# Moving twelve first additions of softmax weights to GpSimd, and folding the second batch's sums once more

## The chip, the cores and the metric

The kernel runs on one core of one Trainium2 chip. The metric is the device time of one execution in microseconds (us); for a kernel that ran several times, the median.

## The reference

Two layers, one after the other. The first is attention with a hash mask for 4 batches, 8 heads, 768 positions and 64 columns per head; the second is a feed-forward layer whose hidden values are the maximum of three products.

```
bits   = (q @ proj > 0), (k @ proj > 0)          # 6 bits each, a bucket per row
scores = q @ k.T / 8, -1e9 where the buckets of query and key differ
attn   = exp(scores - max) / (sum(exp(scores - max)) + 1e-9)
x      = attn @ v, heads side by side            # 3072 x 512
h      = maximum(x @ w1, x @ w2, x @ w3)          # 3072 x 768
out    = h @ w_out                                # 3072 x 512, float32
```

## The kernel before

**Units.** The queries are cut into nine chunks: three of 256 queries for batch 0 (chunks 0, 1, 2), and two of 384 for each of the others (3 and 4 for the second batch, 5 and 6 for the third, 7 and 8 for the fourth). A unit is 768 weights per partition of one chunk and one head: `scores` (line 281) issues its matmuls into PSUM (line 297), and one ScalarE exponential writes the weights in fp16 to one of 24 tiles `AT` (line 305). A chunk of 384 queries has three units per head, n = 0, 1, 2, each with two blocks of 128 keys. There are 192 units in all; units 48 to 95 are the second batch.

**The denominators.** A softmax row needs the sum of its weights over all 768 keys. It is taken by matmuls with a column block of ones (line 357, in `burst`), four heads at a time in four column groups. From chunk 3 on, VectorE first adds weights together in `add` (line 321): the addition n = 1 makes `ad` from the tiles of units 0 and 1 (line 328, `ad<-AT,AT`), the addition n = 2 adds the third tile (line 328, `ad<-ad,AT`), each over 768 columns. For chunks from `THIRD_ADD` on, a third addition puts the two halves of `ad` together, over 384 columns (line 331). `sum_blocks` then hands `burst` one block a head (chunks 5 to 8) or two (chunks 3 and 4). `ad` has five buffers.

**Order.** The order of every engine's queue is written out by hand in the loop over units (line 616). In slot u the kernel issues the scores of unit u + 1, then what `when` has put into the slot, then one or so pieces of the feed-forward layer, then the burst of four heads when one is due. The additions of unit (c, h, n) stand in slot u + 2, after everything else that `when` put there, so the additions n = 1 and n = 2 of one head are one slot apart. A burst of the second batch stands four slots after its last unit.

**The other work of the queues.** The feed-forward pieces use one of four PSUM banks in turn (line 412); VectorE takes them out (line 421, from chunk 3 on line 417 on ScalarE for the first of three products; line 419 before that). VectorE also transposes q and k of coming batches (line 201, `turn`) and makes the reciprocal sums and normalized rows (lines 364 to 386). GpSimd has three kinds of work after the start: it narrows transposed q and k to bf16 (line 206, `narrow`), issues the loads of q and k (line 195) and issues those of v (line 239). SyncE's queue holds the transfers out of the narrowed tiles (`place`) and the output.

Of the kernel before, what the change touches and what calls it, by code (L numbers as in the profile page):

```python
# [12 lines left out]
AluOp = mybir.AluOpType  # L13
# [4 lines left out]
def kernel(  # L18
# [12 lines left out]
    nc = tc.nc  # L31
# [20 lines left out]
    EPS = 2.0 ** -60  # L52
    NAT = 24
    SPREAD = {2: (61, 9), 3: (100, 12)}
    THIRD_ADD = 5
    LAG = (1, 4)
    ATW = 776

# [215 lines left out]
    def blocks(t, w):  # L274
        nb = 2 * HALF // w
        return t[:, 0 : nb * (w + 2)].rearrange("p (n c) -> p n c", n=nb)
# [32 lines left out]
    def weights_of(c, h, m):  # L309
        w = chunks[c][2]  # L310
        nb = 2 * HALF // w
        return blocks(at_tiles[at_of[unit_at[c, h, m // nb]]], w)[:, m % nb, :]
# [6 lines left out]
    sum_of = {}  # L319

    def add(c, h, n):
        w = chunks[c][2]
        t = [blocks(at_tiles[at_of[unit_at[c, h, i]]], w)[:, :, 0:w] for i in range(n + 1)]
        if n == 1:
            sum_of[c, h] = ad_pool.tile([P, 2, HALF], FP16, tag="ad", name="ad")
        else:
            t[0] = sum_of[c, h][:]
        nc.vector.tensor_tensor(out=sum_of[c, h][:], in0=t[0], in1=t[n], op=AluOp.add)  # L328
        if n == 2 and c >= THIRD_ADD:
            t = sum_of[c, h]  # L330
            nc.vector.tensor_tensor(out=t[:, 0, :], in0=t[:, 0, :], in1=t[:, 1, :], op=AluOp.add)  # L331

    def sum_blocks(c, h):
        w = chunks[c][2]
        if (c, h) in sum_of:
            t = sum_of[c, h]
            return [t[:, j, 0:w] for j in range(1 if c >= THIRD_ADD else 2)]
        return [weights_of(c, h, m)[:, 0:w] for m in range(NM)]
# [146 lines left out]
    with tc.manual_schedule():  # L485
# [126 lines left out]
        for u, (c, h, n) in enumerate(units):  # L612
            if c >= 3 and n:
                when(min(u + 2, NU - 1), add, c, h, n)
# [58 lines left out]
```

## Time and profile before

| | before |
|---|---|
| median of 3 runs | 266.32 us (265.26 to 266.48) |
| the profiled execution | 265.27 us, span 263.1 us |
| TensorE (PE) busy | 256.4 us, 97% |
| VectorE (DVE) busy | 208.5 us, 79% |
| ScalarE (ACT) busy | 177.4 us, 67% |
| GpSimd (POOL) busy | 70.1 us, 27% |
| additions of line 328 | 96, on VectorE |
| third additions of line 331 | 32, on VectorE |

An engine's busy time is the time in which at least one of its instructions ran; instructions that follow each other overlap by some hundredths of a microsecond, so start-to-start times are shorter than durations. The profiled execution is one run; its span runs from the first to the last instruction of the program, and its time is 2.2 us longer. The second batch's units run from about 55 to 111 us in the span.

### The profile page before, as it was taken

The page shows a single profiled execution, that of the slowest core. Times are in us where ns is not written, and L with a number is a line of the kernel's source. Part 1 is how long each engine was busy: PE and PEld are TensorE (multiplying, and loading weights), DVE is VectorE, ACT ScalarE, POOL GpSimd, SP SyncE. Part 2 cuts the span into 40 slices and gives each one's busy share as a digit, 9 for nine tenths or more (in the row PEclk, how much of TensorE's full clock was granted, in tenths as well). Part 3 has the DMA queues.
Part 4 walks back from the last instruction along what each step waited for, and adds up shares of the span by engine and source line. Part 5 has one row for each costly group of instructions (what it writes and reads, how often), then busy time and mean ns, then how long its engine had stood idle before and what let it go on. Part 6 is the DMA issues. An engine that isn't in the chain of part 4 may idle for free.

```text
span 263.1 us, 6495 instructions
## 1 busy us (share of the span) xinstructions
PE 256.4 (97%) x2509; PEld 153.6 (58%) x2509; DVE 208.5 (79%) x494; ACT 177.4 (67%) x257; POOL 70.1 (27%) x132
## 2 busy tenths in 40 slices
PE   7999999999999999999999999999999999999994
PEld 3555666866765666555555555555555555554552
DVE  3897766967799999978999997999759795887451
ACT  3697885667968675956869588584886859581322
POOL 4678752355043526331131612011000000000000
PEclk9999999999999999999999999999999999999999
DMA  6999999969832954970073653802030003000303
GB/s 173 306 247 193 173 251 222 203 114 206 207 91 69 205 141 62 268 188 18 0 209 93 119 123 48 208 1 62 15 122 1 0 2 121 2 0 2 120 0 120
DMA packets 20862, 30.95 MB, mean 118 GB/s; under 512 B 2625, under 2 KB 15393, under 8 KB 20833
## 3 DMA queue, kind: packets, MB, share of 16 engines
q0 software_dynamic: 8128, 13.37, 27.1%
q1 hardware_dynamic: 12192, 16.73, 22.0%
q10 hardware_dynamic: 512, 0.46, 0.5%
q8 instruction: 19, 0.31, 0.5%
q14 instruction: 11, 0.08, 0.1%
HBM read 25.17 MB, written 6.29 MB: 120 GB/s over the span
## 4 chain that ended last, share of the span: by engine, by line
PE 88%; DVE 5%; ACT 2%; issue 1%; DMA 1%; POOL 1%; ACTq 0%; DVEq 0%
PE ms L412 34%; PE sc L297 22%; PE ms L460 11%; PE ms L379 10%; PE ms L220 3%; PE ms L357 3%; ACT AT L305 2%; DMA nat<-in_q_dram 1%; PE ms L123 1%; PE ms L170 1%; DVE S L175 1%; DVE ht L421 1%; DVE ad L328 1%; PE ms L150 1%; POOL S L137 1%
## 5 line engine op out<-in xcount | busy, mean ns | idle before, releaser
L305 ACT ACTIVATE AT<-sc 128x768 f16<-128x768 f32 x192 | 152.6, 816 | 59.4 <-PE sc L297 56.1
L412 PE MATMUL ms<-xT,w_sb 128*128 128x384 f16 (+1 forms) x648 | 114.8, 307 | 0.1
L297 PE MATMUL sc<-S 72*128 72x384 bf16 (+1 forms) x432 | 93.6, 308 | 1.6 <-ACT AT L305 0.7
L412 PEld LDWEIGHTS <-w_sb 128*128 128x128 f16 x648 | 62.7, 97 | 35.9 <-issue 0.4
L421 DVE TENSOR_TENSOR ht<-ht,ms 128x384 f16<-128x384 f16 (+1 forms) x108 | 54.2, 503 | 21.7 <-PE ms L412 11.3
L297 PEld LDWEIGHTS <-S 72*128 72x128 bf16 (+1 forms) x432 | 39.4, 98 | 33.7 <-issue 13.5
L206 POOL TENSOR_SCALAR T<-T 128x768 bf16<-128x768 f32 x24 | 22.9, 954 | 90.3 <-issue 47.5
L460 PE MATMUL ms<-wout_sb,ht 128*128 128x512 f16 x138 | 35.5, 378 | 0.0
L379 PE MATMUL ms<-AT,vo 128*32 128x385 f16 (+3 forms) x840 | 34.4, 308 | 0.1
L328 DVE TENSOR_TENSOR ad<-ad,AT 128x768 f16<-128x768 f16 x48 | 26.5, 552 | 2.1 <-ACT AT L305 1.3
L379 PEld LDWEIGHTS <-vo 128*32 128x32 f16 x864 | 22.4, 96 | 9.5 <-issue 1.6
L201 DVE STREAM_TRANSPOSE T<-nat 128x384 f32<-128x384 f32 x48 | 26.8, 563 | 0.0
L328 DVE TENSOR_TENSOR ad<-AT,AT 128x768 f16<-128x768 f16 x48 | 26.2, 545 | 0.2 <-ACT AT L305 0.2
L417 ACT CAST ht<-ms 128x384 f16<-128x384 f32 x36 | 17.3, 480 | 8.1 <-PE ms L412 8.1
L460 PEld LDWEIGHTS <-ht 128*128 128x128 f16 x138 | 13.3, 97 | 13.0 <-issue 0.3
L386 DVE SCALAR_TENSOR_TENSOR xT<-ms,sv,rb 128x384 f16<-128x384 f32 (+1 forms) x35 | 19.2, 565 | 1.3
L464 ACT COPY osb<-ms 128x512 f32<-128x512 f32 x21 | 12.3, 586 | 7.1 <-PE ms L460 5.8
L331 DVE TENSOR_TENSOR ad<-ad 128x384 f16<-128x384 f16 x32 | 15.5, 484 | 1.1
L137 POOL TENSOR_SCALAR S<-T 64x384 bf16<-64x384 f32 (+1 forms) x23 | 14.2, 619 | 5.8 <-DVE T L132 4.4
L364 DVE STREAM_TRANSPOSE ys<-ms 128x384 f32<-128x384 f32 (+1 forms) x17 | 9.0, 531 | 6.3 <-PE ms L357 6.2
L195 POOL DMA_DIRECT2D nat<-in_q_dram x20 | 11.1, 561 | 0.1
L175 DVE TENSOR_SCALAR S<-ms 6x384 bf16<-6x384 f32 x16 | 8.9, 554 | 2.2 <-PE ms L170 1.8
(52 smaller groups left out, 122.1 us busy)
## 6 DMA issues: line engine op xcount, KB each, us to landing
out_dram<-osb SPq DMA_DIRECT2D x21, 256.0 KB
S<-T SPq DMA_DIRECT2D x48, 96.0 KB
nat<-in_q_dram POOLq DMA_DIRECT2D x20, 192.0 KB, 6.4
vo<-in_v_dram POOLq DMA_DIRECT2D x8, 384.0 KB, 5.9
nat<-in_k_dram POOLq DMA_DIRECT2D x16, 192.0 KB, 5.9
w_sb<-in_moe_w_dram POOLq DMA_DIRECT2D x3, 768.0 KB, 12.3
nat<-in_k_dram SPq DMA_DIRECT2D x10, 192.0 KB
nat<-in_k_dram SPq DMA_DIRECT2D x3, 384.0 KB
```

The costliest lines, as they stand in the source:

```text
L137: nc.gpsimd.tensor_scalar(out=o, in0=i_, scalar1=RS, scalar2=1.0, op0=AluOp.mult, op1=AluOp.mult)
L201: nc.vector.transpose(t32[name][:, u, half * HALF : (half + 1) * HALF], i_)
L206: nc.gpsimd.tensor_scalar(out=t16[name][:, u, :], in0=t32[name][:, u, :], scalar1=RS, scalar2=1.0, op0=AluOp.mult, op1=AluOp.mult)
L297: nc.tensor.matmul(views[j], s_of[kn][0 : D + bits, kx, m * P : (m + 1) * P], s_of[qn][0 : D + bits, qx, q0 : q0 + w], start=True, stop=True)
L305: nc.scalar.activation(t[:, :, 0:w], whole, ActFn.Exp, bias=-SCALE * 0.25 * bits, scale=SCALE)
L328: nc.vector.tensor_tensor(out=sum_of[c, h][:], in0=t[0], in1=t[n], op=AluOp.add)
L379: nc.tensor.matmul(av[Q * x : Q * (x + 1), 0:n], v_at[2 * b + i][:, x, cb * D + side : (cb + 1) * D : 2], weights_of(c, 4 * i + x, m)[:, 0 ...
L386: nc.vector.scalar_tensor_tensor(out=xt_of(c)[:, 2 * i + side, 0:w], in0=av[:, 0:w], scalar=sv_of[b, i, side][:], in1=rb[0][:, 0:w], op0=A ...
L412: nc.tensor.matmul(ps[:, 0:w], w_sb[wi][:, jc, fb * P : (fb + 1) * P], xt[:, jc, 0:w], start=(jc == 0), stop=(jc == NJC - 1))
L417: nc.scalar.copy(hts[fb][:, 0:w], ps[:, 0:w])
L421: nc.vector.tensor_tensor(out=hts[fb][:, 0:w], in0=hts[fb][:, 0:w], in1=ps[:, 0:w], op=AluOp.max)
L460: nc.tensor.matmul(ps[:, 0:DM], hts[fb][:, tb * P : (tb + 1) * P], wout_sb[:, fb, :], start=(fb == 0), stop=(fb == NFB - 1))
```

## The change

`THIRD_ADD` becomes 3, so that the sixteen heads of chunks 3 and 4 get the third addition too, and their bursts read one block a head in place of two. In the same chunks, the addition n = 1 of heads 0, 1, 2 and 4, 5, 6 (three of four) goes to GpSimd's queue, in the slot where it stood in VectorE's. The additions n = 2 and the third additions stay on VectorE.

```diff
-    THIRD_ADD = 5
+    THIRD_ADD = 3
...
-        nc.vector.tensor_tensor(out=sum_of[c, h][:], in0=t[0], in1=t[n], op=AluOp.add)
+        eng = nc.gpsimd if n == 1 and c < 5 and h % 4 < 3 else nc.vector
+        eng.tensor_tensor(out=sum_of[c, h][:], in0=t[0], in1=t[n], op=AluOp.add)
         if n == 2 and c >= THIRD_ADD:
             t = sum_of[c, h]
             nc.vector.tensor_tensor(out=t[:, 0, :], in0=t[:, 0, :], in1=t[:, 1, :], op=AluOp.add)
```

## The prediction

> **What bounds the kernel now.** I read the page's busy line first, then the table of stretches for the second batch, then the chain of waits there.
>
> ```profile
> span 263.1 us, 6495 instructions
> PE 256.4 (97%) x2509; PEld 153.6 (58%) x2509; DVE 208.5 (79%) x494; ACT 177.4 (67%) x257; POOL 70.1 (27%) x132
> ```
>
> TensorE is busy for 97% of the span, VectorE for 79%. An average hides stages, so the stretch that the change touches is looked at by itself (columns: length, then busy time and instructions of PE, PEld, DVE, ACT, POOL, the granted clock, the DMA share and GB/s).
>
> ```profile
> 70.00:110.00 40.00, 39.86 (x407) 25.65 (x405) 38.51 (x94) 28.81 (x40) 15.34 (x21) 1.00 0.59 134
> ```
>
> From 70 to 110 us VectorE is busy for 38.51 of 40 us. It has 1.49 us to spare, and TensorE has 0.14. Both are full, at a granted clock of 1.00, and GpSimd is busy for 15.34. The chain that ended last shows which of the two carries the end (columns: start, duration, what):
>
> ```profile
> 98.66 0.44 PE ms L412 x4
> 99.10 0.33 PE sc L297 x2
> 99.43 0.44 PE ms L412 x4
> ```
>
> Here TensorE runs back to back, and a slot with one feed-forward piece takes 99.43 - 98.66 = 0.77 us. So TensorE is the bound, with VectorE just able to follow. A wait put into VectorE's queue is free only as far as the 1.49 us go, plus the lead that the PSUM banks give.
>
> **What TensorE saves.** The four bursts of the second batch lose half of their sum matmuls, eight become four. Both forms are in the trace (columns: start, duration, then engine, line, operation and count): the first pair of rows is a burst of the second batch, the other one of the third.
>
> ```profile
> 73.17 0.51 PE L357 MATMUL ms<-ad,ones 128*32 128x384 f16 x8
> 73.50 2.15 PE L379 MATMUL ms<-AT,vo 128*32 128x385 f16 x48
> ...
> 132.28 0.35 PE L357 MATMUL ms<-ad,ones 128*32 128x384 f16 x4
> 132.45 2.15 PE L379 MATMUL ms<-AT,vo 128*32 128x385 f16 x48
> ```
>
> Start to start, eight take 73.50 - 73.17 = 0.33 us and four take 0.17. Four bursts save 4 x 0.16 = 0.64 us. That is on the path, and it is nearly all that can be won, since TensorE has only 0.14 us of idle time in the stretch.
>
> **What VectorE's own work becomes.** Between 70 and 110 us the trace has these additions, on VectorE:
>
> ```profile
> L328 DVE TENSOR_TENSOR ad<-AT,AT x12: 510/536/552, 70.1 to 109.5; 128x768 f16<-128x768 f16 x12
> L328 DVE TENSOR_TENSOR ad<-ad,AT x11: 515/516/993, 71.4 to 108.1; 128x768 f16<-128x768 f16 x11
> ```
>
> Of the twelve n = 1 additions, three (heads 3 and 7 of chunk 3, head 3 of chunk 4) stay, and nine go to GpSimd. The eleven n = 2 additions stay, and each gets a third addition behind it. What one costs in the queue is read from start to start:
>
> ```profile
> 81.97 0.55 DVE L328 TENSOR_TENSOR ad<-AT,AT 128x768 f16<-128x768 f16 x1
> 82.44 0.41 DVE L421 TENSOR_TENSOR ht<-ht,ms 128x256 f16<-128x256 f16 x1
> ...
> 120.30 0.52 DVE L328 TENSOR_TENSOR ad<-ad,AT 128x768 f16<-128x768 f16 x1
> 120.85 0.36 DVE L331 TENSOR_TENSOR ad<-ad 128x384 f16<-128x384 f16 x1
> 121.13 1.21 DVE L421 TENSOR_TENSOR ht<-ht,ms 128x384 f16<-128x384 f16 x2
> ```
>
> A large addition holds the queue for 0.47 us. One with a third addition behind it holds it for 121.13 - 120.30 = 0.83, so the third one costs 0.36. Removed are 9 x 0.47 = 4.2 us and added are 11 x 0.36 = 4.0. I call that zero: VectorE's queue is as full as before.
>
> **What the GpSimd additions do to VectorE.** The trace has no two-input instruction on GpSimd, but it shows what a one-input one does to VectorE's additions. GpSimd's narrowing alone, and twice beside a VectorE addition:
>
> ```profile
> 36.85 0.83 POOL L206 TENSOR_SCALAR T<-T 128x768 bf16<-128x768 f32 x1 [0.48 <-DVE T L201]
> ...
> 84.75 0.98 POOL L206 TENSOR_SCALAR T<-T 128x768 bf16<-128x768 f32 x1 [2.55 <-issue]
> ...
> 124.19 0.98 POOL L206 TENSOR_SCALAR T<-T 128x768 bf16<-128x768 f32 x1 [10.27 <-issue]
> ```
>
> ```profile
> 84.53 0.52 DVE L328 TENSOR_TENSOR ad<-AT,AT 128x768 f16<-128x768 f16 x1
> 85.15 0.99 DVE L328 TENSOR_TENSOR ad<-ad,AT 128x768 f16<-128x768 f16 x1
> ...
> 124.51 0.86 DVE L331 TENSOR_TENSOR ad<-ad 128x384 f16<-128x384 f16 x1
> ```
>
> The addition at 85.15 meets a GpSimd operation that ends at 85.73, and itself ends at 86.14 after 0.99 us in place of 0.52. The third addition at 124.51 meets one that ends at 125.17, and ends at 125.37 after 0.86 in place of 0.36. In both cases VectorE's addition does its work after the GpSimd operation has ended. The other way round, the narrowing that starts inside the addition at 84.53 takes 0.98 in place of 0.83. The two exclude each other. The group of third additions says how often:
>
> ```profile
> L331 DVE TENSOR_TENSOR ad<-ad 128x384 f16<-128x384 f16 x32 | 15.5, 484 | 1.1
> L331 DVE TENSOR_TENSOR ad<-ad x32: 357/358/866, 120.9 to 238.1; 128x384 f16<-128x384 f16 x32
> ```
>
> Mean 484 against median 358 over 32 is 4.0 us, or eight hits of 0.51.
>
> These rows do not say whether a GpSimd addition with two inputs excludes VectorE's for its whole length. The Trainium skill, SBUF — State Buffer, section "SBUF: two separate sides", says that the pair of ports common to both engines goes to the first comer for a whole instruction, and names VectorE operations with two SBUF inputs among those that block; by that rule the sum below holds, and without it the second rival does.
>
> How long is a GpSimd addition, X? One pass over 768 elements takes 0.83 us. Two inputs read together would also take 0.83, the low end; two passes take 1.66, which I use, as the operation reads twice as much; two passes with the delay of the colliding narrowing, 1.05 at most by the row at 99.90 quoted below, take 2.1, the high end. The Trainium skill, GPSIMD Engine Reference, section "Performance versus the Vector engine", gives 4497 ns for 2048 fp32 elements; an estimate scaled from that is 1.69 us, by which the sum would end 0.3 us higher.
>
> Some encounters can be followed one by one (ScalarE's row is the unit that releases head 4's addition on GpSimd):
>
> ```profile
> 70.16 0.81 ACT L305 ACTIVATE AT<-sc 128x768 f16<-128x768 f32 x1
> ```
>
> ```profile
> 71.40 0.52 DVE L328 TENSOR_TENSOR ad<-ad,AT 128x768 f16<-128x768 f16 x1
> ...
> 80.35 0.52 DVE L328 TENSOR_TENSOR ad<-ad,AT 128x768 f16<-128x768 f16 x1
> ...
> 93.51 0.52 DVE L328 TENSOR_TENSOR ad<-ad,AT 128x768 f16<-128x768 f16 x1
> ...
> 99.74 0.52 DVE L328 TENSOR_TENSOR ad<-ad,AT 128x768 f16<-128x768 f16 x1
> ```
>
> ```profile
> 80.52 1.05 POOL L206 TENSOR_SCALAR T<-T 128x768 bf16<-128x768 f32 x1 [3.85 <-DVE T L201]
> ...
> 92.39 0.59 POOL L195 DMA_DIRECT2D nat<-in_q_dram  x1
> ...
> 99.90 1.05 POOL L206 TENSOR_SCALAR T<-T 128x768 bf16<-128x768 f32 x1 [3.58 <-DVE T L201]
> ```
>
> Head 4 of chunk 3: its weights are there at 70.97, GpSimd is free, and its addition runs until 72.6. Head 3's n = 2 addition, at 71.40 on VectorE, waits 1.2 us for it. Head 1 of chunk 4: GpSimd's queue is held by a narrowing and a load issue until 92.98, so its addition ends at 94.64. VectorE reaches the n = 2 addition that needs the result at 93.51 and waits 1.1 us. Behind VectorE's waiting instruction stand the evacuations of lines 419 and 421; TensorE waits for their banks.
>
> For all of them I take chance encounters. Nine GpSimd additions in 40 us are one every 4.44 us. A VectorE addition that comes at any moment meets one with chance X / 4.44 and waits X / 2 on average. There are 25 of them in the stretch: 3 + 11 + 11. So 25 x 1.66 x 1.66 / (2 x 4.44) = 7.8 us (1.9 for X = 0.83, 12.4 for 2.1).
>
> The new third additions meet narrowings too, 0.51 us each. A narrowing starts inside an n = 2 addition three times in the stretch, the first at 80.52 and the last at 99.90 above; the third addition follows 0.55 us after the second, so it falls inside the narrowing: 1.5 us.
>
> Against these 9.3 us stand VectorE's spare 1.5 us and the banks' lead, which I bound by nothing and by two slots and take as one slot, 0.8 us, once. What is left, 7.0, is lost by TensorE, which has no idle time to give it back.
>
> **Moved and hidden.** GpSimd's loads fall behind additions in its queue. The four at 61.97 move behind two of them, 3.3 us later; the first VectorE transpose that needs them comes 20 us later, with a landing time of 6.4 us.
>
> ```profile
> 61.97 2.19 POOL L195 DMA_DIRECT2D nat<-in_q_dram  x4
> nat<-in_q_dram POOLq DMA_DIRECT2D x20, 192.0 KB, 6.4
> 82.77 0.57 DVE L201 STREAM_TRANSPOSE T<-nat 128x384 f32<-128x384 f32 x1
> ```
>
> If that cover were gone, the price would be the shift itself, 3.3 us. GpSimd's load in the stretch becomes 15.34 + 9 x 1.66 = 30.3 of 40 us, so its queue holds. The transfers of `place` on SyncE's queue only follow the narrowings; five `ad` buffers are enough, as a burst frees four of them while the next head's are made. I cost these at nothing.
>
> **The sum.** 7.8 + 1.5 - 1.5 - 0.8 - 0.6 = +6.4 us. On the profiled execution, 265.27, that gives 271.7; it lies 1.05 below the median of the runs, 266.32, so the median should be 272.7. The ends of X give +0.5 (266.8) and +11.0 (277.3).
>
> **Rivals.** *Half the encounters.* The phases are not random: the additions start when ScalarE has ended, and several find VectorE on evacuations for their whole length. With half of 7.8 the sum is +2.5: 268.8. For it: GpSimd's additions come some two slots before their results are needed. Against: two of the encounters above cost over 1 us each. *No exclusion by two-input additions.* Only waits for results remain, of which the walk above shows 1.1 us, and the spare 1.5 us hide them. Then TensorE's saving stands alone: 265.7, not slower. The case decides itself where all of VectorE's new waits stay under 1.5 + 0.8 = 2.3 us. Against it are the eight hits of 0.51. *GpSimd becomes the late one.* With X of 2.1 and more its load passes 34 of 40 us, narrowings come late, and every n = 2 addition waits for its first: 277.3 or above. Against it: a one-input pass takes 0.83. That the edit reaches other heads than said is excluded by its conditions: lines 328 and 331 count 96 and 32 before, and must count 84 on VectorE plus 12 on GpSimd, and 48.
>
> **How the numbers follow.** The forecast has 0.62, half the encounters 0.17, no exclusion 0.13, a late GpSimd 0.08. The range from 267.0 to 276.5 holds the first two, and leaves out the last two, 0.21. A measurement tells about 0.5%, or 1.33 us, from no change: no exclusion counts as the same (0.12) but for a small part that measures faster (0.02); the rest is slower (0.86).
>
> **What would show it.** In the profile after, twelve GpSimd additions of about 1.7 us; VectorE additions beside them that last 1 to 2.5 us; VectorE's busy share in the second batch at its full, and TensorE's idle time there up by 6 to 7 us; the bursts' sum matmuls in fours. I am wrong if the additions of line 328 on VectorE keep their 0.52 us beside GpSimd's, or if TensorE's idle time stays under 1 us.

## The result and the profile after

The changed kernel takes 276.93 us (median; 276.29 to 277.11), the kernel before on the same chip 266.09. The ratio is 1.040, 95% interval 1.038 to 1.043: 10.8 us slower. The forecast was 272.7 with a range from 267.0 to 276.5, so the direction was right and the size was not: the sum said +6.4, and the range ended 0.4 us too low.

Line numbers behind the edit are one higher in the changed kernel: line 329 is the large addition, 332 the third one, 413 and 422 the feed-forward matmuls and their evacuation. The page's first lines, and the same stretch as before (length, then busy time and instructions of PE, PEld, DVE, ACT, POOL, the granted clock, the DMA share, GB/s):

```profile
span 275.3 us, 6484 instructions
PE 261.1 (95%) x2493; PEld 155.6 (57%) x2493; DVE 219.9 (80%) x498; ACT 177.4 (64%) x257; POOL 89.3 (32%) x144
```

```profile
70.00:110.00 40.00, 34.16 (x296) 21.84 (x296) 36.61 (x80) 22.02 (x29) 19.87 (x21) 0.91 0.38 93
```

TensorE, at 39.86 of 40 us before, stands for 5.84 us in this stretch, and its granted clock is 0.91 where it was 1.00. VectorE is busy for 36.61 us, not fuller than before as forecast: it now waits too. By the start of each unit's exponential, all of the loss lies between units 60 and 96; from unit 104 on the two kernels keep a constant distance.

The additions by instruction (minimum, median and maximum in ns):

```profile
L329 DVE TENSOR_TENSOR ad<-ad,AT x48: 507/548/1984, 64.2 to 249.7; 128x768 f16<-128x768 f16 x48
L329 DVE TENSOR_TENSOR ad<-AT,AT x36: 515/551/1297, 72.6 to 249.1; 128x768 f16<-128x768 f16 x36
L329 POOL TENSOR_TENSOR ad<-AT,AT x12: 1632/1648/1709, 62.5 to 121.3; 128x768 f16<-128x768 f16 x12
...
L332 DVE TENSOR_TENSOR ad<-ad x48: 357/358/2450, 66.2 to 250.3; 128x384 f16<-128x384 f16 x48
```

The edit did what it says: 84 large additions on VectorE, 12 on GpSimd, 48 third ones. A GpSimd addition takes 1.65 us. VectorE's additions reach 1.98, 1.30 and 2.45 us.

The costliest episode, on GpSimd's queue, on VectorE's, and on TensorE's (whose first two rows are from another place, the first burst):

```profile
97.41 1.03 POOL L206 TENSOR_SCALAR T<-T 128x768 bf16<-128x768 f32 x1 [2.88 <-DVE T L201]
98.51 0.58 POOL L195 DMA_DIRECT2D nat<-in_q_dram  x1
99.11 3.24 POOL L329 TENSOR_TENSOR ad<-AT,AT 128x768 f16<-128x768 f16 x2
```

```profile
100.80 1.98 DVE L329 TENSOR_TENSOR ad<-ad,AT 128x768 f16<-128x768 f16 x1 [0.47 <-POOL ad L329]
```

```profile
75.93 0.35 PE L358 MATMUL ms<-ad,ones 128*32 128x384 f16 x4 [1.06 <-DVE ht L420]
76.55 3.71 PE L380 MATMUL ms<-AT,vo 128*32 128x385 f16 x48 [0.27 <-DVE ht L422]
...
103.56 0.95 PE L413 MATMUL ms<-xT,w_sb 128*128 128x256 f16 x4 [2.40 <-DVE ht L422]
```

A narrowing and a load issue hold GpSimd's queue, so two additions run back to back from 99.11 to 102.35. VectorE waits for the first one's result, and the second has begun when it comes: its addition starts at 100.80 and ends at 102.78, 0.43 us after GpSimd's. TensorE has no free bank and stands for 2.40 us. What follows such a stand is in the table by single microseconds (the granted clock is the figure third from the end):

```profile
78.00:79.00 1.00, 1.00 (x19) 0.55 (x12) 0.90 (x4) 0.00 (x0) 0.94 (x3) 0.50 0.00 0
...
102.00:103.00 1.00, 0.00 (x0) 0.00 (x0) 0.97 (x2) 0.07 (x1) 0.35 (x1) 1.00 0.28 74
...
105.00:106.00 1.00, 1.00 (x6) 0.70 (x5) 0.97 (x4) 0.76 (x1) 0.24 (x1) 0.50 0.06 16
```

In this execution TensorE's clock is halved for some 3.4 us, once around 78 and once around 105. The forty-eight matmuls of line 380 take 3.71 us in the first of these, where they took 2.15.

### The profile page after: what moved, and what is told of

Its sections match the earlier page's. It is cut to its first block, busy times and chain, and to the rows that moved or that the text cites. A ratio compares the mean times of both kernels' runs of the same rounds, so it can differ in the third digit from the quotient of the medians.

```text
span 275.3 us, 6484 instructions
## 1 busy us (share of the span) xinstructions
PE 261.1 (95%) x2493; PEld 155.6 (57%) x2493; DVE 219.9 (80%) x498; ACT 177.4 (64%) x257; POOL 89.3 (32%) x144
## 4 chain that ended last, share of the span: by engine, by line
PE 80%; DVE 9%; issue 3%; ACT 3%; POOL 2%; DMA 1%; ACTq 0%; DVEq 0%; POOLq 0%
PE ms L413 31%; PE sc L297 20%; PE ms L380 11%; PE ms L461 9%; DVE ad L329 3%; PE ms L220 3%; PE ms L358 3%; ACT AT L305 3%; DVE ad L332 1%; DMA nat<-in_q_dram 1%; POOL ad L329 1%; PE ms L123 1%; PE ms L170 1%; DVE S L175 1%; DVE T L201 1%
## 5 line engine op out<-in xcount | busy, mean ns | idle before, releaser
L413 PE MATMUL ms<-xT,w_sb 128*128 128x384 f16 (+1 forms) x648 | 116.1, 310 | 4.8 <-DVE ht L422 3.5
L422 DVE TENSOR_TENSOR ht<-ht,ms 128x384 f16<-128x384 f16 (+1 forms) x108 | 54.2, 503 | 21.4 <-PE ms L413 10.3
L380 PE MATMUL ms<-AT,vo 128*32 128x385 f16 (+3 forms) x840 | 36.0, 318 | 0.7 <-DVE rr L368 0.4
L329 DVE TENSOR_TENSOR ad<-ad,AT 128x768 f16<-128x768 f16 x48 | 29.1, 606 | 3.8 <-POOL ad L329 2.0
L380 PEld LDWEIGHTS <-vo 128*32 128x32 f16 x864 | 23.7, 99 | 11.6 <-issue 3.9
L332 DVE TENSOR_TENSOR ad<-ad 128x384 f16<-128x384 f16 x48 | 27.2, 567 | 1.6
L329 DVE TENSOR_TENSOR ad<-AT,AT 128x768 f16<-128x768 f16 x36 | 20.5, 569 | 0.2 <-ACT AT L305 0.2
L329 POOL TENSOR_TENSOR ad<-AT,AT 128x768 f16<-128x768 f16 x12 | 19.7, 1652 | 2.6 <-ACT AT L305 2.4
## 6 DMA issues: line engine op xcount, KB each, us to landing
w_sb<-in_moe_w_dram POOLq DMA_DIRECT2D x3, 768.0 KB, 11.4
```

The source lines that it names most:

```text
L329: eng.tensor_tensor(out=sum_of[c, h][:], in0=t[0], in1=t[n], op=AluOp.add)
L380: nc.tensor.matmul(av[Q * x : Q * (x + 1), 0:n], v_at[2 * b + i][:, x, cb * D + side : (cb + 1) * D : 2], weights_of(c, 4 * i + x, m)[:, 0 ...
L413: nc.tensor.matmul(ps[:, 0:w], w_sb[wi][:, jc, fb * P : (fb + 1) * P], xt[:, jc, 0:w], start=(jc == 0), stop=(jc == NJC - 1))
L422: nc.vector.tensor_tensor(out=hts[fb][:, 0:w], in0=hts[fb][:, 0:w], in1=ps[:, 0:w], op=AluOp.max)
```

## The experiments

Times are medians of a run's kernel against the kernel before on the same chip, with the ratio's interval. The runs were made on several chips, so two of them are compared by their distances from their own kernel before. The code cuts leave out the lines that make a spare tile or constants; in e3, e4, e8 and e12 the tile `ys` also has one buffer in place of two. The theory: GpSimd additions shut out VectorE's, VectorE gets late, TensorE stands. Its rivals: the third additions are the trouble (A), the waits for GpSimd's results (B), GpSimd's late queue (C).

**e1, the third additions alone.**

```diff
-    THIRD_ADD = 5
+    THIRD_ADD = 3
```

> The third additions of chunks 3 and 4 alone, all additions on VectorE. Exclusion theory (the loss comes from GpSimd additions that shut out VectorE's): VectorE gets 11 x 0.36 = 4.0 us more work between 70 and 110 us and up to 1.5 us of meetings with the narrowing, against 1.5 us to spare and one slot of lead, 0.8; minus 0.6 of saved matmuls: +2 to +3 us, and no lowered clock. Rival A (the third additions are the trouble, the place of the first additions is not): +8 us or more, most of the change's +10.8. Rival B (the waits for GpSimd's results): as before or below it, -0.6 to +1.

271.24 against 265.74, ratio 1.020 (1.017 to 1.023): +5.5 us, twice what the theory allowed, at a clock of 0.998. Neither it nor rival A had the size. VectorE cannot take 0.36 us more per head.

**e2, the GpSimd additions alone** (the diff without its first line).

> The twelve first additions on GpSimd, no third additions in chunks 3 and 4. Exclusion theory: 14 VectorE additions in place of 25 can be hit between 70 and 110 us, so 14/25 of 7.8 = 4.3 us, while VectorE is relieved of 9 x 0.47 = 4.2: -0.5 to +2 us. Rival A (third additions): 0 or below. Rival B (waits for GpSimd's results): the same two or three waits as in the full change remain, so +5 us or more.

271.67, ratio 1.021 (1.018 to 1.024): +5.9 us. VectorE has less work than before, and the kernel is slower all the same. The two halves add up to 11.4 us, about the whole change's 10.8. Rival B is not excluded by this run. (Expectations below carry the two results as +5.3 and +5.5, by their ratios.)

**e3, twelve GpSimd additions on top of the kernel before, results unused.**

```diff
         nc.vector.tensor_tensor(out=sum_of[c, h][:], in0=t[0], in1=t[n], op=AluOp.add)
+        if n == 1 and c < 5 and h % 4 < 3:
+            nc.gpsimd.tensor_tensor(out=spare[:], in0=t[0], in1=t[n], op=AluOp.add)
```

> The kernel before, with twelve GpSimd additions on top, of the same inputs in the same slots, into a tile that nobody reads. VectorE keeps all its additions, nobody waits for a result; one buffer of a small tile that only VectorE uses is given up for space. Exclusion theory: VectorE has 23 additions to be hit between 70 and 110 us, 23/25 of 7.8 = 7.1 us, no relief; minus 2.3 of slack and lead: +5 us, and more, up to +9, if TensorE's clock falls in the waits. Rival B (waits for results): within 0.5 us of the kernel before.

276.02, ratio 1.039 (1.035 to 1.042): +10.3 us, with nobody waiting for a result. VectorE's additions by instruction:

```profile
L329 DVE TENSOR_TENSOR ad<-AT,AT x48: 511/551/2794, 61.9 to 247.9; 128x768 f16<-128x768 f16 x48
L329 DVE TENSOR_TENSOR ad<-ad,AT x48: 509/548/1665, 64.2 to 248.6; 128x768 f16<-128x768 f16 x48
```

Maxima of 2.79 and 1.67 us, where the kernel before has 0.99. Rival B falls as the main cause.

**e4, fills in place of the extra additions.**

```diff
+        if n == 1 and c < 5 and h % 4 < 3:
+            for _ in range(4):
+                nc.gpsimd.memset(spare[:], 0.0)
```

> The kernel before, with four GpSimd fills of about 0.4 us in each of the same twelve slots, into a tile that nobody reads: GpSimd is held for about 1.6 us each time, but reads nothing. Exclusion theory, in the form that GpSimd has to read to shut VectorE out: within 1 us of the kernel before. Rival C (GpSimd's queue comes late, so that loads and narrowings do): as the kernel with the extra additions, +5 us or more.

266.39, ratio 1.003 (1.000 to 1.006): +0.7 us. The page's group and VectorE's additions:

```profile
L332 POOL MEMSET spare<- 128x500 f32 x48 | 24.9, 518 | 2.2
```

```profile
L329 DVE TENSOR_TENSOR ad<-AT,AT x48: 516/551/979, 62.2 to 238.4; 128x768 f16<-128x768 f16 x48
L329 DVE TENSOR_TENSOR ad<-ad,AT x48: 510/533/995, 63.0 to 239.0; 128x768 f16<-128x768 f16 x48
```

GpSimd is held for 24.9 us (0.52 a fill, not the 0.4 expected), more than the 20.6 of the twelve additions in e3, with the same loads and narrowings behind, and VectorE's additions keep their lengths of before. So an occupied GpSimd queue costs little (rival C), and a GpSimd operation that reads costs much.

**e5, the loads of the last two batches on SyncE's queue.**

```diff
-    when(us[0] - 14 + x, load_quad, side, g, (x,), nc.gpsimd)
+    when(us[0] - 14 + x, load_quad, side, g, (x,), nc.sync)
```

> The whole change, but the loads of q and k for the third and fourth batch are issued on SyncE's queue in place of GpSimd's. If part of the loss comes from load issues ahead of an addition (they delay it, so that two additions run back to back, and VectorE is shut out from their start on), this gains 2 to 5 us on the whole change: 272 to 275, no VectorE addition waits beyond the rows of GpSimd's additions, and at least one of the two stretches of lowered clock is gone. If only the additions' own length counts: within 1 us of the whole change, 276 to 277.

275.26, ratio 1.034 (1.027 to 1.041): +9.5 us, 1.4 less than the whole change, with an interval that runs from no gain to more than 3 us. In the profiled execution one stretch of halved clock is left of two. By the median, the load issues are a smaller part of it than the 2 us set as the mark; a wait beyond an addition's row remained too, behind an issue for v, which was not moved.

**e6, one head of four on GpSimd.**

```diff
-    eng = nc.gpsimd if n == 1 and c < 5 and h % 4 < 3 else nc.vector
+    eng = nc.gpsimd if n == 1 and c < 5 and h % 4 < 1 else nc.vector
```

> The whole change with one head of four on GpSimd in place of three (four additions, never two in a row). Exclusion theory, from the third additions alone (+5.3): relief of 3 x 0.47 = 1.4 between 70 and 110 us, against 28 additions that can be hit by three GpSimd additions, 28 x 1.66 x 1.66 / (2 x 13.3) = 2.9: +6 to +7.5, 272 to 273, at a clock of 1.00. If GpSimd's share were what relieves VectorE, it would lie above the whole change's +10.8.

273.37, ratio 1.028 (1.020 to 1.037): +7.6 us at a clock of 1.00, just above the range expected. By the medians that is between e1 and the whole change: each step of more GpSimd additions costs more than it relieves.

**e7, small matmuls in TensorE's gaps.**

```diff
+            for _ in range({63: 14, 82: 36}.get(u, 0)):
+                nc.tensor.matmul(bank_tiles[3][:, 384:512], ones16[:, :], ones16[:, :], start=True, stop=True)
             credit += 1 if u < UPB else 1.15
```

> The whole change with small matmuls of constants put where TensorE stands idle, 14 in slot 63 ahead of the first burst and 36 in slot 82, 0.05 us each. Theory that the lowered clock is the price of the idle time before it: the granted clock stays at 1.00 in the stretches that had 0.83, and the time falls by 1.7 us for each one avoided, 273 to 275.5. Rival (the clock falls for another reason): clock near 0.986 again and the time the same or up to 2.7 us longer.

280.33, ratio 1.053 (1.046 to 1.060), where 273 to 275.5 was expected: the second half failed as an experiment, since those 36 waited for a bank themselves (3.52 us of standing ahead of them) and then ran at half clock. The first fourteen ran in the gap, and the first stretch of halved clock was gone. e11 keeps only these.

**e8 and e12, one long stall of VectorE in the kernel before.**

```diff
+        when(170, nc.vector.memset, spare[:], 0.0)
+        for _ in range(10):        # e12: 16
+            when(175, nc.vector.transpose, spare[:], spare[:])
```

> The kernel before with ten VectorE transposes of a spare tile, about 0.5 us each, in a row in slot 175: one stall of about 5 us, of which the banks' lead takes about 2. Theory: TensorE idles for about 3 us, its clock is halved afterwards for some 3.4 us, and the time grows by 3 + 1.7, 4 to 5.5 us. Without a tie between idling and clock: 3 us or less.

> The kernel before with sixteen VectorE transposes of a spare tile in a row in slot 175, 9.7 us in all, where ten (6.1 us) cost TensorE 1.3 us of idle time and no clock. Theory: TensorE stands 4.5 to 5 us in one piece, and the clock is halved afterwards for some 3.4 us, 1.7 us more: +6 to +7.5 us on the kernel before. Without a tie: +4.5 to +5.5.

e8 takes 267.64 (+1.9 us, where 4 to 5.5 was expected), e12 272.47 (+6.9 us). VectorE's stall, TensorE's gap behind it, and for e12 the table after the gap:

```profile
217.45 6.09 DVE L484 STREAM_TRANSPOSE spare<-spare 128x384 f32<-128x384 f32 x10
```

```profile
226.41 0.81 PE L413 MATMUL ms<-xT,w_sb 128*128 128x384 f16 x4 [1.03 <-DVE ht L422]
```

```profile
216.28 9.77 DVE L484 STREAM_TRANSPOSE spare<-spare 128x384 f32<-128x384 f32 x16
```

```profile
228.93 1.44 PE L413 MATMUL ms<-xT,w_sb 128*128 128x384 f16 x4 [4.72 <-DVE ht L422]
```

```profile
231.00:232.00 1.00, 1.00 (x5) 0.44 (x3) 0.90 (x3) 0.81 (x1) 0.00 (x0) 0.50 0.00 0
```

Ten transposes leave a gap of 1.03 us and the clock at full: TensorE ran on through about 5 us of the stall, which I put down to the banks and to room in the queue, where I had allowed 2. Sixteen leave 4.72 us, and the clock is halved behind it. The tie between standing and clock is shown. The Trainium skill, TensorE: Matmul & The Clock Gate, section "The HAM clock gate", describes this gate with a full and a half rate; the rows, at 1.00 and 0.50, agree.

**e9, the whole change without its GpSimd additions.**

```diff
+        if c < 5 and h % 4 < 3:
+            if n == 1:
+                return
+            t[0] = t[1]
...
-                nc.vector.tensor_scalar(out=rr[:, 0:n], in0=ys[:, 0:w:Q], scalar1=EPS * S, scalar2=None, op0=AluOp.add)
+                nc.vector.tensor_scalar(out=rr[:, 0:n], in0=ys[:, 0:w:Q], scalar1=EPS * S if b != 1 else 1.0, scalar2=None, op0=AluOp.add)
```

> The whole change with the twelve GpSimd additions left out: for those heads the addition n = 2 adds the second and third unit's weights, so the first unit's are missing from the denominators of the second batch, and 1 is added to these. VectorE's work and the saved matmuls are as in the whole change. Theory (the whole loss is what the twelve GpSimd additions do to VectorE): the time of the kernel before, minus at most 0.6 and plus up to 1.5 us for third additions that meet a narrowing, 265 to 267.5. Rival A (the third additions are too much even so): half of the loss stays, 270 to 272.

This kernel leaves the first unit's weights out of the denominators of those heads. 268.75, ratio 1.012 (1.009 to 1.016): +3.2 us. The expectation missed. The GpSimd additions account for the other 10.84 - 3.15 = 7.7 us of the change, but third additions cost over 3 us even when VectorE gets rid of twelve large ones for nothing. One of the places, on VectorE's queue and then on TensorE's: a third addition (line 336 here) that meets a narrowing takes 0.87 us in place of 0.36, and TensorE stands for 0.80 us behind it.

```profile
81.24 0.87 DVE L336 TENSOR_TENSOR ad<-ad 128x384 f16<-128x384 f16 x1
```

```profile
82.49 0.60 PE L417 MATMUL ms<-xT,w_sb 128*128 128x256 f16 x4 [0.80 <-DVE ht L426]
```

**e10, e2 with one GpSimd addition taken back.**

```diff
-        eng = nc.gpsimd if n == 1 and c < 5 and h % 4 < 3 else nc.vector
+        eng = nc.gpsimd if n == 1 and c < 5 and h % 4 < 3 and (c, h) != (4, 1) else nc.vector
```

> The GpSimd additions without the third ones (+5.5 us there), but the second head of chunk 4 keeps its first addition on VectorE, so that no two GpSimd additions run back to back around 95 us. There TensorE stood for 2.89 us and then ran at half clock for some 3.4 us. Theory (the loss comes in few episodes, and lowered clock follows a long one): 4 us or more of the 5.5 are gone, 266 to 267.5, clock 1.00. Rival (loss in proportion to the number of additions): 1/12 of it goes, 270.5 to 271.

268.66, ratio 1.012 (1.009 to 1.015). TensorE's rows around the spot, first of e2, then of e10:

```profile
99.22 0.60 PE L413 MATMUL ms<-xT,w_sb 128*128 128x256 f16 x4 [2.89 <-DVE ht L422]
```

```profile
98.23 0.60 PE L413 MATMUL ms<-xT,w_sb 128*128 128x256 f16 x4 [1.31 <-DVE ht L422]
```

One addition of twelve takes 2.9 of e2's 5.9 us with it, less than the 4 expected and far more than its share. The gap shrinks by 1.58 us, and the halved clock behind it is gone; the loss comes in episodes.

**e11, the fourteen small matmuls of e7 alone.**

> The whole change with the fourteen small matmuls of constants in slot 63 alone. The first stretch of lowered clock, 76 to 80 us, should go, and with it 1.7 to 2.3 us of the time: 274.5 to 275.5, mean clock 0.992 to 0.994. If the clock's fall is not tied to idling: 276.5 to 278.

276.49, ratio 1.041 (1.037 to 1.045): +10.9 us, as much as the whole change. Yet the forty-eight matmuls run at full clock:

```profile
75.85 2.16 PE L381 MATMUL ms<-AT,vo 128*32 128x385 f16 x48 [0.27 <-DVE ht L423]
```

TensorE reaches unit 65 some 1.5 us earlier than in the whole change, and by unit 72 is no earlier: VectorE was late, and TensorE waited for it instead. Here the halved clock had cost nothing, since TensorE was not the one waited for.

**e13 to e16, what third additions cost.** e13 is e9 without third additions; e13 and e14 leave out the same weights as e9. e14, e15 and e16 put every addition ahead of the other work of its slot, in e9, in e1 and in the kernel before:

```diff
-                when(min(u + 2, NU - 1), add, c, h, n)
+                at.setdefault(min(u + 2, NU - 1), []).insert(n - 1 if u + 2 >= NU - 1 else 0, lambda c=c, h=h, n=n: add(c, h, n))
```

> VectorE's relief alone: the twelve first additions of the second batch left out and nothing put in their place (the first unit's weights are missing from those denominators, 1 is added to them), no third additions. VectorE has 5.6 us less to do. If VectorE was not what TensorE waited for in the kernel before, this is worth nothing: 265 to 266, within 0.6 us of it. If VectorE was, several us are gained.

> As the whole change with the GpSimd additions left out (268.75), with every addition put ahead of the other work of its slot, so that a narrowing starts beside evacuations and not inside an addition. If what is left there (+3.1) comes from third additions that meet narrowings: 265 to 266.5. If it comes from the third additions' own time in the full queue: 268 to 269.

> The third additions alone, all on VectorE (+5.3 before), again with every addition ahead of the other work of its slot. Meetings as the cause: about 1.5 to 3 us less, 268 to 269.7. Own time as the cause: 270.5 to 271.5.

> The kernel before with every addition ahead of the other work of its slot. Ten VectorE additions that meet a narrowing (0.5 us each) no longer should; TensorE did not wait for them, so the time stays within 0.6 us of the kernel before.

e13: 265.60, ratio 1.000 (0.997 to 1.002). Its stretch:

```profile
70.00:110.00 40.00, 40.00 (x408) 25.81 (x406) 35.38 (x86) 28.95 (x40) 17.07 (x24) 1.00 0.56 134
```

VectorE is busy for 35.38 us where it was 38.51, TensorE for all 40.00, and the time is the same: relief of VectorE alone had nothing to win. e14: 266.75, ratio 1.004 (1.003 to 1.006); e15: 269.46, ratio 1.014 (1.013 to 1.016); e16: 265.53, ratio 0.998 (0.996 to 1.001). Taking most of the meetings with narrowings away gains 2.1 us in e9, 1.7 in e1 and nothing in the kernel before. So meetings are the larger part of what is left in e9, and the third additions' own time is the rest: 1.1 us, or 1.7 with the saved matmuls counted. Without VectorE's relief, in e15, their own time is the larger part, 3.8 us. Where in the queue the own time is lost was not taken apart. No version beats the kernel before by an amount that can be told.

## Why the prediction was wrong

**The mechanism was right.** Two-input GpSimd additions take the time that was put for X (1.66 put, 1.65 measured), and the VectorE additions that met one in the rows above end 0.2 or 0.4 us after it. *No exclusion* falls by e3 against e4, *half the encounters* by the result. *A late GpSimd*: the time came close to its 277.3, but not in its way, since X is 1.65 and e4 shows a held queue to cost 0.7 us.

**The step "VectorE's own work becomes zero, and 1.5 + 0.8 us of slack and lead stand against the meetings" failed.** By it, the change without GpSimd additions would be 1.5 - 2.3 - 0.6 = -1.4, so no slower than before; e9 measured +3.2. That is 4.6 us too low, as much as the whole miss of 4.4, since the GpSimd additions, put at 7.8, measured 7.7. In the terms of the sum, by e9 and e14: the narrowings cost 2.1 in place of 1.5, and VectorE's own work, with whatever slack and lead there was, cost 1.7, where nothing less 2.3 was put. The wash of 4.2 against 4.0 us is one of totals. e13 shows VectorE's relief to be worth nothing by itself, e1 that about as much work on top costs 5.5; beside third additions the relief is worth 2.3 (e1 against e9). That what is removed lies in other slots than what is added, and VectorE's spare time elsewhere again, is my reading of this, and not shown slot by slot. One place can be seen: the prediction read the chain of the kernel before at 98.66 us, but the same chain runs through VectorE from 69.77 to 81.25:

```profile
69.77 0.42 DVE ht L421
...
80.87 0.34 DVE ht L421
81.25 0.60 PE ms L412 x4
```

There VectorE had no reserve, and e1 loses its first 1.9 us at the end of it, between units 68 and 72. The lead of the banks did not help either, as the rows of e9 show.

**A term was missing, the clock, but it is not the miss.** The sum charged TensorE's standing and not what follows it. In the profiled execution the standing came out near its term: 7.3 us between 55 and 130 us, where 7.0 was put. Most of the rest there is TensorE's own work, which the two stretches of halved clock lengthen by 3.71 - 2.15 = 1.6 us and by about as much around 105. But a full clock would not have saved this. The four executions of the changed kernel took 277.11 and 277.00 us at a mean granted clock of 0.986, 276.85 at 0.992 and 276.29 at 0.998, a difference of 0.8 us at most. Two executions of e11 had a mean of 1.00, and took 276.38 and 276.33, still 10.7 us more than the kernel before. In e11's profile TensorE stands for 7.8 us: standing takes the place of the halved clock, since VectorE is late. It can be otherwise: in e10 a gap with its clock is worth 2.9 us, 1.58 of it by the gap, and I put the rest down to the clock.

**The meetings were placed wrongly, and the 7.8 is in part luck.** I counted them from 70 us on. In the part of the changed kernel that answers to that stretch, 72 to 121 us, GpSimd's additions lengthen VectorE's rows and waits by 5.6 us where 7.8 was put: 0.8 at 72.59, 1.4 at 90.78, 1.9 at 100.80 with the wait ahead of it, and 1.5 at 113.13, in a row of the reciprocal that the count did not have. The narrowings add 2.5, 0.9 of which the kernel before has too, close to the 1.5 put. Another 4.4 us came before 70 us, which the sum did not count: 1.45 in the addition at 64.21 with 0.9 of waiting ahead of it, and 2.1 in this third addition:

```profile
65.71 1.09 POOL L195 DMA_DIRECT2D nat<-in_q_dram  x2
66.81 1.65 POOL L329 TENSOR_TENSOR ad<-AT,AT 128x768 f16<-128x768 f16 x1
```

```profile
66.23 2.45 DVE L332 TENSOR_TENSOR ad<-ad 128x384 f16<-128x384 f16 x1
```

They left VectorE with no reserve when the full stretch began.

**What held.** The saved matmuls: four rows of x4, as forecast. The loads behind the additions: no transpose waits for one there, and their place ahead of additions is worth 1.4 us by e5, not told from nothing.

## What to carry to other kernels

Where one engine is full and another only just keeps up with it, count the follower's work slot by slot: a wash of totals hides the places where the leader will stand. Before work is moved to GpSimd, ask which VectorE instructions run beside it, since additions on the two engines shut each other out, and ask whether TensorE's clock falls behind a stand: in e10 that seems to have cost nearly as much as the stand, in the changed kernel 0.8 us at most, since VectorE was late anyway. And ask first what the relief is worth, by leaving the work out: here it was worth nothing by itself.

## What the runs showed of the hardware

A short VectorE operation with one input is shut out as well. The reciprocal's first step works on 12 elements, takes 0.17 us, and took 1.66 beside a GpSimd addition:

```profile
112.98 1.65 POOL L329 TENSOR_TENSOR ad<-AT,AT 128x768 f16<-128x768 f16 x1
```

```profile
113.13 1.66 DVE L367 TENSOR_SCALAR rr<-ys 128x12 f32<-128x12 f32 x1
```

GpSimd fills, which shut out no addition in e4, did hold this one, for 0.4 us:

```profile
88.35 2.25 POOL L332 MEMSET spare<- 128x500 f32 x4
```

```profile
88.94 0.55 DVE L370 TENSOR_SCALAR rr<-ys 128x12 f32<-128x12 f32 x1
```

The Trainium skill, SBUF — State Buffer, section "SBUF: two separate sides", makes that distinction: two-input VectorE operations against GpSimd operations that read, the two-port forms against any. Whether the reciprocal's step is such a form, no row says.

A VectorE addition can be shut out before GpSimd's row begins: the one at 66.23 above starts while GpSimd issues loads, with an addition queued behind them, and ends 0.2 us after that addition. Another, at 90.78, also starts beside load issues with an addition behind them, and takes 1.73 us, but ends 0.2 us after the issues; why the two differ is open. The kernel before has additions beside load issues that keep their length.

TensorE's clock fell without one long gap: before the first stretch it stood for 0.4, 1.1 and 0.3 us within 3 us. A single gap of 1.31 us, in e10, left it at full. It does not fall in every execution of one kernel, as the mean clocks of 0.986 to 0.998 show.
